# Attention scores as float32 products on quarters of the TensorE array, with queries and keys stored once

## The chip, the core and the metric

The kernel runs on one core of a Trainium2 chip. The metric is the device time of one execution in microseconds (us); lower is better. The core has a matrix engine (TensorE, PE in the profile; its weight loads are PEld), VectorE (DVE), ScalarE (ACT), GpSimd (POOL) and SyncE (SP), which issues the DMAs.

## What is computed

Windowed causal attention with a linear bias, and then a two-matrix feed-forward block on its output. B = 8 batches, H = 8 heads, S = 576 positions, D = 64; the feed-forward part has 4608 tokens, 512 features and 2048 inner features.

```python
scores = scale * np.matmul(q, k.transpose(0, 1, 3, 2))
mask = (rel >= 0) & (rel < 128)
scores = np.where(mask, scores + bias[None], -1000000000.0)
attn = softmax(scores)                      # over keys
x = np.matmul(attn, v)                      # heads joined: 4608 x 512
h = x @ w_in
g = h * erf(np.maximum(h, 0.0) + np.log1p(np.exp(-np.abs(h))))
return g @ w_out
```

## The kernel before

**A planner orders everything.** Each piece of work is an `op` with a cost per engine that may take it, the buffers that it reads and writes, and a due time `at`. `Plan.run` simulates the engines and the buffer slots and picks, on each engine, the ready op with the smallest due time. The kernel is emitted in that order. So a changed cost or buffer changes the order of all the work around it.

**Attention** runs as 48 spans: 12 chunks `c` of positions times 4 pairs of heads `g`. Every third chunk (16 spans, `w` = 1, the second kind) takes the last 192 positions of two batches; the other 32 spans (`w` = 0, the first kind) take 384 positions of one batch. A span has three tiles of 128 queries (two halves of 64). Each half sees three blocks of 64 keys (192 columns), in the first tile of a first-kind span two (128 columns).

- `operands` (DMA at L387) loads the span's queries and keys. Queries of the two halves lie on the diagonal of a 128x128 matrix whose other half is zeros, one such matrix for each head; the keys of half 0 lie on partitions 0 to 63, those of half 1 on 64 to 127. A key block that several tiles need is stored several times: 1792 or 1920 columns.
- `scores` (L422) makes two full-array products for each tile, one for each head, in float32, into one PSUM bank. VectorE adds the bias table and takes the row minimum of the negated scores (`biased`, L434), ScalarE takes the exponential and the sum (`exps`, L442).
- `normalise` divides (L465, GpSimd; VectorE too in the first four spans). `transpose_bank` transposes the probabilities on TensorE (L485), two banks a first-kind span and three a second-kind one, with a copy of each to SBUF (L403 on ScalarE, L407 on VectorE). `av` multiplies by the values into `px` (L501), and `px` is copied out by the same two lines and stored.

PSUM has eight banks: one each for scores (`s`), transposes (`t`) and `px` (`x`), and five that belong to the feed-forward part (`h` twice, `o0` to `o2`). In the first eight spans (`n < SPARE`) the scores of a tile take `s` or the two `h` in turn, and every second transposed bank takes `o1`.

**The feed-forward part** runs in two passes over the inner features. The first (7 of 16 blocks of weights) is interleaved with the attention, whose output it takes chunk by chunk; the second starts when the attention's SBUF memory has been given back. L694 makes `h`, L765 makes `o`; each product is split into three of a faster float format (high and low parts). L731 and L733 are its ScalarE functions. The weights are prepared on ScalarE and VectorE (L570 to L591). Warm-up products (L374) have the last due time and fill gaps on TensorE in the first microseconds.

Of the kernel before, what the change touches and what calls it, by code (L numbers as in the profile page):

```python
# [8 lines left out]
F32 = mybir.dt.float32  # L9
# [9 lines left out]
NPAIR = H // 2  # L19
P = 128  # L20
# [21 lines left out]
PB, XB, OB, TB = 8, 3, 3, 4  # L42
QB, VB = 4, 2

TE, NE = 2.0, 28
TA = 1.8
LL, LP, LT = 15, 6, 0
# [11 lines left out]
    [(2, 128), (3, 0), (3, 0)],  # L59
    [(3, 0), (3, 0), (3, 0)],  # L60
]
BANKS = [
# [5 lines left out]
]  # L68
VALUES = [
# [239 lines left out]
def dma(nbytes, n=1, us=0.475):  # L309
    return dict(costs={"SP": n * us}, moved=nbytes)  # L310
# [19 lines left out]
class Attention:  # L330
# [46 lines left out]
    def operands(self, c, g, w, at):  # L377

        op, sync, n = self.plan.op, self.nc.sync.dma_start, self.n
        x = Buf(self.qkp, [P, 1920], F32, "qk", QB, f"qk{n}")  # L380
        pos, parts = [0], []
        for blocks, _ in TILES[w]:
            pos.append(pos[-1] + 256 + 128 * blocks)
            parts.append(Part(x, slice(None), slice(pos[-2], pos[-1])))
        for a, b in ((0, 1), (1, 2), (2, 3)) if n < 2 else ((0, 3),):
            at += 0.01 * a
            op(emit=lambda e, a=pos[a], b=pos[b]: sync(x[:, a:b], self.src_qk[c, g, :, a:b]), w=parts[a:b], at=at,  # L387
               **dma(P * (pos[b] - pos[a]) * 4))
        self.loaded.append(Buf(ap=True))
        self.loaded[-1].writer = self.plan.ops[-1]  # L390
        return parts

    def values(self, c, g, w, at):

# [11 lines left out]
        else:  # L406
            self.nc.vector.tensor_copy(out, src)  # L407

    def scores(self, g, w, t, x, low, total, at):
        nc, op = self.nc, self.plan.op  # L410
        blocks, c0 = TILES[w][t]
        n = 64 * blocks
        nm = f"{self.n}_{t}"
        ways = [(self.ps, "s", 1)]
        if self.n < SPARE and t < 3:
            ways += [(self.spare[0], "h", 2)] * 2
        pool, tag, bufs = ways[self.step % len(ways)]
        ps = Buf(pool, [P, 2, 256], F32, tag, bufs, f"s{nm}")

        def products(e):  # L420
            for j in range(2):
                nc.tensor.matmul(  # L422
                    ps[:, j, :n], lhsT=x[:, j * P : (j + 1) * P], rhs=x[:, 2 * P + j * n : 2 * P + (j + 1) * n],
                    start=True, stop=True,
                )

        op({"PE": 2 * fp32_us(n)}, products, r=[x], w=[ps], at=at)
        pt = Buf(self.pp, [P, 3, 2, 64], F32, "p", PB, f"p{nm}")
        cut = lambda x: x.rearrange("p (c d) -> p c d", d=64)
        table = self.tables[g]  # L430

        def biased(e):
            for j in range(2):
                nc.vector.tensor_tensor_reduce(  # L434
                    out=pt[:, :blocks, j, :], in0=cut(ps[:, j, :n]), in1=cut(table.ap[:, j * 256 + c0 : j * 256 + c0 + n]),
                    scale=-0.125, scalar=3.0e38, op0=ALU.add, op1=ALU.min, accum_out=low[:, j : j + 1],
                )
# [7 lines left out]
        op({"DVE": 2 * (dve(n) + 0.05)}, biased, r=[ps, table], w=[pt, low], at=at)  # L445
        op({"Act": 2 * (act(n, 1) + 0.09)}, exps, r=[pt, low], w=[pt, total], at=at)
        return pt

# [60 lines left out]
    def span(self, c, g):  # L509
        op, n = self.plan.op, self.n  # L510
        w = int(c % 3 == 2)
        at = step_time(self.step) - LL + 0.01 * n
        x = self.operands(c, g, w, at)
        v = self.values(c, g, w, step_time(self.step) - LL + (VA if n < AHEAD else 2))
        p, totals = [], []
        st = Buf(self.pp, [P, 12], F32, "st", 4, f"st{n}")
        for t in range(3):
            at = step_time(self.step)
            low, total = (Part(st, slice(None), slice(k, k + 2)) for k in (2 * t, 6 + 2 * t))
            p.append(self.scores(g, w, t, x[t], low, total, at))  # L520
            totals.append(total)
            self.step += 1
        self.normalise(w, p, st, totals, at)
        at += LT
        sb = [Buf(self.ptp, [P, 512], F32, "pa", TB, f"pa{n}_{x}") for x in range(len(BANKS[w]))]
        for bi in range(len(BANKS[w])):
            self.transpose_bank(w, bi, p, sb, at)
        px = Buf(self.ps, [P, 512], F32, "x", 1, f"px{n}")
        for step in range(len(VALUES[w])):
            self.av(w, step, px, v, sb, at + 0.1)  # L530
        if c < DIRECT:
            xs = Part(self.moe.direct(c), slice(None), g, slice(0, CH))
# [321 lines left out]
def _layout(q, k, v, moe_w_in, moe_w_out):  # L854
    import numpy as np

    nb = q.shape[0]
    heads = lambda a: a.transpose(0, 1, 3, 2).reshape(nb, NPAIR, 2, D, S // 64, 64)
    qh, kh = heads(q), heads(k)
    vh = v.reshape(nb, NPAIR, 2, S // 64, 64, D)  # L860
    nc = 3 * nb // 2
    qk = np.zeros((nc, NPAIR, 2, D, 1920), q.dtype)
    vb = np.zeros((nc, NPAIR, 2, 64, 10, 2, D), v.dtype)
    for c in range(nc):
        x, y = 2 * (c // 3), 2 * (c // 3) + 1
        if c % 3 < 2:
            b = x + c % 3
            tiles = [((b, 2 * t, (2 * t - 1, 2 * t - 2, 2 * t)), (b, 2 * t + 1, (2 * t - 1, 2 * t + 1, 2 * t)))
                     for t in range(3)]
            tiles[0] = ((b, 0, (0, None)), (b, 1, (0, 1)))  # L870
            values = [(b, kb) for kb in range(6)]
        else:
            tiles = [((b, 6, (5, 4, 6)), (b, 7, (5, 7, 6))) for b in (x, y)]
            tiles.append(((x, 8, (7, 6, 8)), (y, 8, (6, 8, 7))))
            values = [(b, kb) for b in (x, y) for kb in range(4, 9)]
        pos = 0
        for halves in tiles:
            size = 64 * len(halves[0][2])
            for half, (b, qb, kbs) in enumerate(halves):
                for j in range(2):  # L880
                    at = pos + (2 * j + half) * 64
                    qk[c, :, half, :, at : at + 64] = qh[b, :, j, :, qb]
                    for n, kb in enumerate(kbs):
                        if kb is not None:
                            at = pos + 256 + j * size + n * 64
                            qk[c, :, half, :, at : at + 64] = kh[b, :, j, :, kb]
            pos += 256 + 2 * size
# [8 lines left out]
    rel = np.concatenate([  # L896
        r + 64 - col, np.where(low, r + 128, r - 64) - col, r - col, np.where(low, -1, r - 64 - col),
    ], axis=1)
    bias = np.where((rel >= 0) & (rel < WIN), -4.0 * rel, -1e30)
    bias = np.concatenate([bias, bias / 2], axis=1).astype(np.float32)  # L900
    return {
        "qk": qk.reshape(nc, NPAIR, P, 1920), "v_b": vb.reshape(nc, NPAIR, P, 10, P), "w_in": wi.reshape(NF, P, DM),
        "w_out": wo.reshape(NF, P, DM), "bias": bias,
    }

# [17 lines left out]
```

## Time and profile before

| | |
|---|---|
| time, median of 3 runs | 1044.85 us (1044.11 to 1045.27) |
| profiled execution | 1045.25 us |
| its span | 1043.1 us |
| TensorE busy | 1031.8 us, 99% |
| ScalarE, VectorE, GpSimd busy | 61%, 53%, 14% |
| DMA traffic | 141.22 MB |

A busy share is the union of an engine's recorded instructions. TensorE's instructions overlap in the record, since it is pipelined and their ends are modelled; so the distance from start to start tells what one of them takes in a row, and its recorded duration tells more than that. "Idle before" a group, or a wait, names what was released last. The chain that ended last is followed back from the last instruction: at each step to what released it, or to the instruction before it on its engine.

### The profile page before, as it was taken

The page shows a single profiled execution, that of the slowest core. Times are in us where ns is not written, and L with a number is a line of the kernel's source. Part 1 is how long each engine was busy: PE and PEld are TensorE (multiplying, and loading weights), DVE is VectorE, ACT ScalarE, POOL GpSimd, SP SyncE. Part 2 cuts the span into 40 slices and gives each one's busy share as a digit, 9 for nine tenths or more (in the row PEclk, how much of TensorE's full clock was granted, in tenths as well). Part 3 has the DMA queues.
Part 4 walks back from the last instruction along what each step waited for, and adds up shares of the span by engine and source line. Part 5 has one row for each costly group of instructions (what it writes and reads, how often), then busy time and mean ns, then how long its engine had stood idle before and what let it go on. Part 6 is the DMA issues. An engine that isn't in the chain of part 4 may idle for free.

```text
span 1043.1 us, 15075 instructions
## 1 busy us (share of the span) xinstructions
PE 1031.8 (99%) x5444; PEld 912.8 (88%) x5444; DVE 550.1 (53%) x1347; ACT 641.1 (61%) x1304; POOL 147.4 (14%) x274
## 2 busy tenths in 40 slices
PE   9999999999999999999999999999999999999998
PEld 8998999899999999999998888888888888888886
DVE  6989655535536535648237963443443535344252
ACT  6979965756755756758468866354454544535462
POOL 0633414323323223300000100000000000000000
PEclk9999999999999999999999999999999999999999
DMA  9987785545565464344112511213030303212011
GB/s 358 390 296 261 249 286 170 194 153 193 201 196 185 144 209 137 124 159 134 56 61 72 172 61 41 81 41 108 14 122 1 121 17 105 71 51 81 0 61 41
DMA packets 52697, 141.22 MB, mean 135 GB/s; under 512 B 5136, under 2 KB 20496, under 8 KB 52624
## 3 DMA queue, kind: packets, MB, share of 16 engines
q1 hardware_dynamic: 52624, 140.27, 39.6%
q8 instruction: 43, 0.70, 0.3%
q14 instruction: 30, 0.25, 0.1%
HBM read 111.94 MB, written 28.31 MB: 134 GB/s over the span
## 4 chain that ended last, share of the span: by engine, by line
PE 81%; ACT 9%; DVE 4%; DMA 2%; POOL 2%; issue 1%; SPq 0%; DVEq 0%; POOLq 0%; ACTq 0%
PE o L765 34%; PE h L694 32%; PE px L501 6%; PE s L422 5%; PE t L485 3%; ACT p L442 2%; POOL p L465 2%; ACT s L731 1%; ACT s L733 1%; ACT L733 1%; ACT L731 1%; ACT L735 1%; DMA xr<-xd 1%; DMA wro<-w_out 1%; ACT pa L403 1%
## 5 line engine op out<-in xcount | busy, mean ns | idle before, releaser
L694 PE MATMUL h<-xh,whi 128*128 128x384 f32 (+1 forms) x660 | 246.4, 373 | 0.3 <-ACT hs L676 0.3
L694 PE MATMUL h<-xh,wli 128*128 128x384 f32 (+1 forms) x660 | 239.4, 363 | 0.0
L694 PE MATMUL h<-xl,whi 128*128 128x384 f32 (+1 forms) x660 | 239.0, 362 | 0.0
L765 PE MATMUL o<-who,gh 128*128 128x512 f32 x576 | 234.4, 407 | 0.1
L765 PE MATMUL o<-who,gl 128*128 128x512 f32 x576 | 225.5, 392 | 0.0
L765 PE MATMUL o<-wlo,gh 128*128 128x512 f32 x576 | 225.2, 391 | 0.0
L676 ACT COPY hs<-h 128x384 f32<-128x384 f32 (+2 forms) x130 | 59.5, 468 | 237.4 <-PE h L694 237.2
L465 POOL TENSOR_SCALAR p<-p,st 128x192 f32<-128x192 f32 (+1 forms) x264 | 142.0, 557 | 299.4 <-DVE st L456 161.1
L442 ACT ACTIVATE p<-p,st 128x192 f32<-128x192 f32 (+1 forms) x288 | 124.8, 437 | 41.4 <-DVE st L434 41.0
L434 DVE CUSTOM_DVE_ANT_0 p<-s,tables 128x192 f32<-128x192 f32 (+1 forms) x288 | 86.1, 338 | 105.3 <-PE s L422 97.1
L694 PEld LDWEIGHTS h<-xh,whi 128*128 128x128 f32 x660 | 124.2, 188 | 15.4 <-ACT hs L676 0.7
L694 PEld LDWEIGHTS h<-xl,whi 128*128 128x128 f32 x660 | 124.2, 188 | 14.5
L694 PEld LDWEIGHTS h<-xh,wli 128*128 128x128 f32 x660 | 123.9, 188 | 12.6
L680 DVE COPY hs<-h 128x512 f32<-128x512 f32 (+2 forms) x63 | 36.4, 578 | 179.5 <-PE h L694 161.9
L765 PEld LDWEIGHTS o<-who,gl 128*128 128x128 f32 x576 | 108.2, 188 | 23.1
L765 PEld LDWEIGHTS o<-who,gh 128*128 128x128 f32 x576 | 108.4, 188 | 18.8 <-DVE ot L680 0.5
L765 PEld LDWEIGHTS o<-wlo,gh 128*128 128x128 f32 x576 | 108.5, 188 | 18.4
L422 PE MATMUL s<-qk 128*128 128x192 f32 (+1 forms) x576 | 111.3, 319 | 2.6 <-DMA qk<-qk 1.4
L501 PE MATMUL px<-pa,v 128*128 128x192 f32 (+2 forms) x704 | 107.2, 296 | 0.0
L501 PEld LDWEIGHTS px<-pa,v 128*128 128x128 f32 x704 | 103.2, 191 | 1.5 <-issue 0.3
L743 DVE TENSOR_TENSOR hs<-s,hs 128x768 f32<-128x768 f32 (+1 forms) x106 | 90.8, 887 | 21.4 <-ACT s L733 21.4
L422 PEld LDWEIGHTS s<-qk 128*128 128x128 f32 x576 | 90.1, 191 | 7.0 <-DMA qk<-qk 1.9
(58 smaller groups left out, 1040.8 us busy)
## 6 DMA issues: line engine op xcount, KB each, us to landing
qk<-qk SPq DMA_DIRECT2D x30, 896.0 KB, 6.6
qk<-qk SPq DMA_DIRECT2D x16, 960.0 KB, 6.8
v<-v_b SPq DMA_DIRECT2D x32, 384.0 KB, 4.5
xr<-xd SPq DMA_DIRECT2D x16, 768.0 KB, 4.9
v<-v_b SPq DMA_DIRECT2D x16, 640.0 KB, 4.4
pd<-ot SPq DMA_DIRECT2D x36, 256.0 KB, 4.6
ot<-pd SPq DMA_DIRECT2D x36, 256.0 KB, 3.4
wri<-w_in SPq DMA_DIRECT2D x16, 512.0 KB, 4.9
```

What stands on the lines that cost most here:

```text
L422: nc.tensor.matmul(ps[:, j, :n], lhsT=x[:, j * P : (j + 1) * P], rhs=x[:, 2 * P + j * n : 2 * P + (j + 1) * n], start=True, stop=True,)
L434: nc.vector.tensor_tensor_reduce(out=pt[:, :blocks, j, :], in0=cut(ps[:, j, :n]), in1=cut(table.ap[:, j * 256 + c0 : j * 256 + c0 + n]), s ...
L442: nc.scalar.activation(dst, dst, AF.Exp, bias=low[:, j : j + 1], scale=-1.0, accum_out=total[:, j : j + 1])
L465: (nc.vector if e == "DVE" else nc.gpsimd).tensor_scalar(dst, dst, totals[t][:, j : j + 1], 1.0, op0=ALU.mult, op1=ALU.mult)
L485: nc.tensor.matmul(cut[:, a : b + 1 : b - a], lhsT=p[t][:, kb].rearrange("p j d -> p (j d)"), rhs=self.ident[:, :], is_transpose=True, sta ...
L501: self.nc.tensor.matmul(dst[:, to : to + size], lhsT=v[:, blk], rhs=sb[s][:, off : off + size], start=(step + n == 0), stop=(last and n == ...
L676: self.nc.scalar.copy(out, src)
L680: self.nc.vector.tensor_copy(out, src)
L694: nc.tensor.matmul(ps[:, :W], lhsT=ww[:, cs], rhs=xx[:, k], start=(k2 + k + n == 0), stop=(k2 + k + n == 4),)
L731: A.activation(s[:, :n], hs[:, :n], AF.Softplus)
L743: op({"DVE": dve(n)}, lambda e, s=s, hs=hs, n=n: V.tensor_tensor(hs[:, :n], s[:, :n], hs[:, :n], ALU.mult), r=[s, hs], w=[hs], at=at)
L765: nc.tensor.matmul(po.all, lhsT=gg[:, cs], rhs=w.all, start=(u["start"] and n == 0), stop=(u["end"] and n == 2),)
```

## The change

Queries and keys are stored once for each span (768 or 1024 columns), head 0 of the pair on partitions 0 to 63 and head 1 on 64 to 127. A score product takes 64 partitions (one head) and 64 queries (one half): head and half choose a quarter of the array. The two heads of a tile write to two banks, the two halves to partitions 0 to 63 and 64 to 127 of each. Where the three key blocks of a half aren't neighbours in the right order, its product is cut into two segments of 64 and 128 columns. The order of the key blocks in a tile is adapted (`BANKS`, the bias table).

All three tiles of a first-kind span are one op of TensorE with one pair of banks; a second-kind span has two such ops (two tiles, then one), each with its pair; the first two spans have one op for each tile. The planner charges such an op `TURN` = 0.34 and half of what the streaming of its columns was charged before. The score banks are now two (`s` with two slots; two `h` for every second span among the first eight). `px` loses its own bank: it takes `o0` in the first eight spans and after that the bank `t` of the transposes.

```diff
+TURN, TS = 0.34, 0.0
+QUERIES = [(128, 0, 640), (0, 128, 256)]
+PIECES = [[(128, 384)], [(0, 128), (384, 512)], [(512, 768)]]
+KEYS = [
+    [[[(256, 0, 2)], [(256, 0, 2)]],
+     [[(256, 0, 3)], [(448, 0, 1), (320, 1, 2)]],
+     [[(384, 0, 3)], [(576, 0, 1), (448, 1, 2)]]],
...
+GROUPS = [[(0, 1, 2)], [(0, 1), (2,)]]
...
     def operands(self, c, g, w, at):
...
-        x = Buf(self.qkp, [P, 1920], F32, "qk", QB, f"qk{n}")
...
-        for a, b in ((0, 1), (1, 2), (2, 3)) if n < 2 else ((0, 3),):
...
+        size = 1024 if w else 768
+        x = Buf(self.qkp, [P, 1024], F32, "qk", QB, f"qk{n}")
+        pieces = PIECES if n < 2 else [[(0, size)]]
...
-    def scores(self, g, w, t, x, low, total, at):
+    def scores(self, w, x, ready, at):
+
+        nc, op = self.nc, self.plan.op
+        tiles = []
+        groups = [(0,), (1,), (2,)] if self.n < 2 else GROUPS[w]
+        banks = None
+        for group in groups:
+            if banks is None or w:
+                pool, tag = self.ps, "s"
+                if self.n < SPARE and self.n % 2:
+                    pool, tag = self.spare[0], "h"
+                banks = [Buf(pool, [P, 512], F32, tag, 2, f"s{self.n}_{group[0]}_{j}") for j in range(2)]
+                pos = 0
+            new = []
+            for t in group:
+                n = 64 * TILES[w][t][0]
+                new.append([Part(b, slice(None), slice(pos, pos + n)) for b in banks])
+                pos += n
+
+            def products(e, group=group, new=new):
+                for t, part in zip(group, new):
+                    q0 = QUERIES[w][t]
+                    for half, segments in enumerate(KEYS[w][t]):
+                        rows = slice(64 * half, 64 * half + 64)
+                        for k0, to, n in segments:
+                            for j in range(2):
+                                d = slice(64 * j, 64 * j + 64)
+                                nc.tensor.matmul(
+                                    part[j].all[rows, 64 * to : 64 * (to + n)],
+                                    lhsT=x[d, q0 + 64 * half : q0 + 64 * half + 64], rhs=x[d, k0 : k0 + 64 * n],
+                                    start=True, stop=True,
+                                )
+
+            op({"PE": TURN + sum(2 * (64 * TILES[w][t][0] / 1200.0 + 0.003) for t in group)}, products,
+               r=ready[group[-1]], w=[p for y in new for p in y], at=at + TS * group[0])
+            tiles += new
+        return tiles
+
+    def softmax(self, g, w, t, ps, low, total, at):
...
-        ways = [(self.ps, "s", 1)]
-        if self.n < SPARE and t < 3:
-            ways += [(self.spare[0], "h", 2)] * 2
-        pool, tag, bufs = ways[self.step % len(ways)]
-        ps = Buf(pool, [P, 2, 256], F32, tag, bufs, f"s{nm}")
-
-        def products(e):
-            for j in range(2):
-                nc.tensor.matmul(
-                    ps[:, j, :n], lhsT=x[:, j * P : (j + 1) * P], rhs=x[:, 2 * P + j * n : 2 * P + (j + 1) * n],
-                    start=True, stop=True,
-                )
-
-        op({"PE": 2 * fp32_us(n)}, products, r=[x], w=[ps], at=at)
...
     def span(self, c, g):
...
-        px = Buf(self.ps, [P, 512], F32, "x", 1, f"px{n}")
+        pool, tag = (self.spare[1], "o0") if n < SPARE else (self.ps, "t")
+        px = Buf(pool, [P, 512], F32, tag, 1, f"px{n}")
```

## Rows read from the trace of the kernel before

**Rows 1.** The page, parts 1 and 2: engines, and slices of TensorE and DMA.
```profile
PE 1031.8 (99%) x5444; PEld 912.8 (88%) x5444; DVE 550.1 (53%) x1347; ACT 641.1 (61%) x1304; POOL 147.4 (14%) x274
...
PE   9999999999999999999999999999999999999998
...
DMA  9987785545565464344112511213030303212011
```

**Rows 2.** The page, part 4: the chain that ended last, by engine and line.
```profile
PE 81%; ACT 9%; DVE 4%; DMA 2%; POOL 2%; issue 1%; SPq 0%; DVEq 0%; POOLq 0%; ACTq 0%
PE o L765 34%; PE h L694 32%; PE px L501 6%; PE s L422 5%; PE t L485 3%; ACT p L442 2%; POOL p L465 2%; ACT s L731 1%; ACT s L733 1%; ACT L733 1%; ACT L731 1%; ACT L735 1%; DMA xr<-xd 1%; DMA wro<-w_out 1%; ACT pa L403 1%
```

**Rows 3.** Windows: stretch, its length, busy time by engine, clock, DMA.
```profile
core 0: us, PE busy (x) PEld busy (x) DVE busy (x) ACT busy (x) POOL busy (x), PEclk, DMA share, GB/s
0.00:25.00 25.00, 22.44 (x153) 21.55 (x154) 15.39 (x92) 15.72 (x54) 0.70 (x6) 1.00 0.93 355
25.00:50.00 25.00, 24.60 (x175) 24.06 (x173) 23.40 (x100) 24.77 (x87) 14.62 (x27) 1.00 1.00 393
...
200.00:250.00 50.00, 49.18 (x299) 45.31 (x298) 26.47 (x97) 32.89 (x97) 19.93 (x36) 1.00 0.52 171
...
700.00:800.00 100.00, 100.00 (x443) 82.86 (x442) 43.84 (x58) 48.20 (x59) 0.00 (x0) 1.00 0.19 64
```

**Rows 4.** The chain in order of time, first 115 us: start, length, what.
```profile
0.74 0.40 SPq L387
...
11.11 1.78 PE warm_ps L374 x16
...
25.96 4.17 ACT p L442 x20
...
58.46 6.93 DMA wro<-w_out
...
102.51 7.37 DMA xr<-xd
```

**Rows 5.** Windows of line 422 alone: stretch, length, PE and PEld busy.
```profile
0.00:100.00 100.00, 31.55 (x167) 25.37 (x168) 1.00 0.89 325
```

**Rows 6.** The chain in order of time, 112 to 200 us.
```profile
131.56 0.44 PE t L485 x4
132.00 0.45 PE s L422 x4
...
134.27 1.69 PE px L501 x12
...
138.85 0.65 PE s L422 x4
```

**Rows 7.** Timeline of TensorE's products from 212.5 us: start, recorded length, what.
```profile
212.61 0.82 PE L422 MATMUL s<-qk 128*128 128x192 f32 x4
213.13 0.47 PE L694 MATMUL h<-xh,whi 128*128 128x384 f32 x1
213.44 0.34 PE L694 MATMUL h<-xl,whi 128*128 128x384 f32 x1
```

**Rows 8.** Line 422: min/median/max duration in ns, first and last start.
```profile
L422 PE MATMUL s<-qk x576: 270/326/430, 4.2 to 436.5; 128*128 128x192 f32 x128, 128*128 128x128 f32 x64
```

**Rows 9.** Timeline of all engines from 181.1 us; these products have 64 columns, then 128.
```profile
181.00 0.97 PEld L501 LDWEIGHTS px<-pa,v 128*128 128x128 f32 x8
```

**Rows 10.** Groups by line and shape: count, busy us, mean ns, idle before.
```profile
L434 DVE CUSTOM_DVE_ANT_0 p<-s,tables 128x192 f32<-128x192 f32 x224 | 70.5, 353 | 90.6 <-PE s L422 83.9 <-PE t L485 3.2 <-POOL p L465 2.7
...
L403 ACT COPY pa<-t 128x512 f32<-128x512 f32 x32 | 18.7, 586 | 10.5 <-PE t L485 10.4
...
L403 ACT COPY xs<-px 128x384 f32<-128x384 f32 x29 | 13.8, 476 | 31.2 <-PE px L501 27.6 <-issue 2.1 <-ACT p L442 1.1
```

**Rows 11.** Waits of TensorE's loads: us in total, times, longest.
```profile
PEld t L485 <- POOL p L465: 3.3, 7, 1.1
PEld t L485 <- ACT pa L403: 3.0, 7, 0.9
```

**Rows 12.** The page, part 6: DMA issues, KB each, us to landing.
```profile
qk<-qk SPq DMA_DIRECT2D x30, 896.0 KB, 6.6
qk<-qk SPq DMA_DIRECT2D x16, 960.0 KB, 6.8
```

More of the change, by code (lines that the diff above doesn't have):

```diff
@@ L61 @@
 ]
-BANKS = [
[5 rows of a table removed]
+QUERIES = [(128, 0, 640), (0, 128, 256)]
+PIECES = [[(128, 384)], [(0, 128), (384, 512)], [(512, 768)]]
+KEYS = [
[6 rows of a table added]
+]
+GROUPS = [[(0, 1, 2)], [(0, 1), (2,)]]
+BANKS = [
[5 rows of a table added]
 ]
@@ L379, in operands @@
         op, sync, n = self.plan.op, self.nc.sync.dma_start, self.n
-        x = Buf(self.qkp, [P, 1920], F32, "qk", QB, f"qk{n}")
[L381 to L384, printed above, removed]
-        for a, b in ((0, 1), (1, 2), (2, 3)) if n < 2 else ((0, 3),):
-            at += 0.01 * a
-            op(emit=lambda e, a=pos[a], b=pos[b]: sync(x[:, a:b], self.src_qk[c, g, :, a:b]), w=parts[a:b], at=at,
-               **dma(P * (pos[b] - pos[a]) * 4))
+        size = 1024 if w else 768
+        x = Buf(self.qkp, [P, 1024], F32, "qk", QB, f"qk{n}")
+        pieces = PIECES if n < 2 else [[(0, size)]]
+        parts = []
+        for k, piece in enumerate(pieces):
+            parts.append([Part(x, slice(None), slice(a, b)) for a, b in piece])
+            for (a, b), part in zip(piece, parts[-1]):
+                op(emit=lambda e, a=a, b=b: sync(x[:, a:b], self.src_qk[c, g, :, a:b]), w=[part],
+                   at=at + 0.01 * min(k, 1) + 0.01 * (k > 1), **dma(P * (b - a) * 4))
         self.loaded.append(Buf(ap=True))
         self.loaded[-1].writer = self.plan.ops[-1]
-        return parts
+        return x, [[p for y in parts[: k + 1] for p in y] for k in range(3)]
     def values(self, c, g, w, at):
@@ L434, in biased @@
                 nc.vector.tensor_tensor_reduce(
-                    out=pt[:, :blocks, j, :], in0=cut(ps[:, j, :n]), in1=cut(table.ap[:, j * 256 + c0 : j * 256 + c0 + n]),
+                    out=pt[:, :blocks, j, :], in0=cut(ps[j].all), in1=cut(table.ap[:, j * 256 + c0 : j * 256 + c0 + n]),
                     scale=-0.125, scalar=3.0e38, op0=ALU.add, op1=ALU.min, accum_out=low[:, j : j + 1],
@@ L443, in exps @@
                     dst, dst, AF.Exp, bias=low[:, j : j + 1], scale=-1.0, accum_out=total[:, j : j + 1])
-        op({"DVE": 2 * (dve(n) + 0.05)}, biased, r=[ps, table], w=[pt, low], at=at)
+        op({"DVE": 2 * (dve(n) + 0.05)}, biased, r=[*ps, table], w=[pt, low], at=at)
         op({"Act": 2 * (act(n, 1) + 0.09)}, exps, r=[pt, low], w=[pt, total], at=at)
@@ L512, in span @@
         at = step_time(self.step) - LL + 0.01 * n
-        x = self.operands(c, g, w, at)
+        x, ready = self.operands(c, g, w, at)
         v = self.values(c, g, w, step_time(self.step) - LL + (VA if n < AHEAD else 2))
@@ L516, in span @@
         st = Buf(self.pp, [P, 12], F32, "st", 4, f"st{n}")
+        ps = self.scores(w, x, ready, step_time(self.step))
         for t in range(3):
@@ L519, in span @@
             low, total = (Part(st, slice(None), slice(k, k + 2)) for k in (2 * t, 6 + 2 * t))
-            p.append(self.scores(g, w, t, x[t], low, total, at))
+            p.append(self.softmax(g, w, t, ps[t], low, total, at))
             totals.append(total)
@@ L861, in _layout @@
     nc = 3 * nb // 2
-    qk = np.zeros((nc, NPAIR, 2, D, 1920), q.dtype)
+    qk = np.zeros((nc, NPAIR, 2, D, 1024), q.dtype)
     vb = np.zeros((nc, NPAIR, 2, 64, 10, 2, D), v.dtype)
@@ L867, in _layout @@
             b = x + c % 3
-            tiles = [((b, 2 * t, (2 * t - 1, 2 * t - 2, 2 * t)), (b, 2 * t + 1, (2 * t - 1, 2 * t + 1, 2 * t)))
-                     for t in range(3)]
-            tiles[0] = ((b, 0, (0, None)), (b, 1, (0, 1)))
+            order = [(qh, b, 2), (qh, b, 3), (qh, b, 0), (qh, b, 1), *((kh, b, n) for n in range(6)), (qh, b, 4), (qh, b, 5)]
             values = [(b, kb) for kb in range(6)]
         else:
-            tiles = [((b, 6, (5, 4, 6)), (b, 7, (5, 7, 6))) for b in (x, y)]
-            tiles.append(((x, 8, (7, 6, 8)), (y, 8, (6, 8, 7))))
+            order = [(qh, x, 6), (qh, x, 7), (qh, y, 6), (qh, y, 7), (qh, x, 8), (qh, y, 8)]
+            order += [(kh, b, n) for b in (x, y) for n in range(4, 9)]
             values = [(b, kb) for b in (x, y) for kb in range(4, 9)]
[L876 to L887, printed above, removed]
+        for n, (src, b, block) in enumerate(order):
+            qk[c, :, :, :, n * 64 : n * 64 + 64] = src[b, :, :, :, block]
         for n, (b, kb) in enumerate(values):
@@ L896, in _layout @@
     rel = np.concatenate([
-        r + 64 - col, np.where(low, r + 128, r - 64) - col, r - col, np.where(low, -1, r - 64 - col),
+        np.where(low, r + 128, r - 64) - col, r + 64 - col, r - col, np.where(low, -1, r - 64 - col),
     ], axis=1)
@@ L901, in _layout @@
     return {
[L902 removed]
+        "qk": qk.reshape(nc, NPAIR, P, 1024), "v_b": vb.reshape(nc, NPAIR, P, 10, P), "w_in": wi.reshape(NF, P, DM),
         "w_out": wo.reshape(NF, P, DM), "bias": bias,
```

13 rows, old and new, of tables (BANKS, KEYS) are left out of this document.

## Prediction

> **What bounds the kernel now.** I read the page's engine shares and slices first [rows 1]. TensorE is busy 1031.8 us of a 1043.1 us span and its line of slices holds nines and a last eight; VectorE and ScalarE stand near 60%. Busy time of a pipelined engine can hide gaps, so the chain that ended last comes next [rows 2]: 81% of it is TensorE, and the scores (L422) are 5% of the span in it. The windows then separate the stages [rows 3]. From 200 us to 800 us TensorE is full and no other computing engine is above two thirds. In the first 50 us it is different: the DMA share is 0.93 and 1.00, and ScalarE is busy 24.77 of 25 us in the second window. The chain in order of time says the same of the start [rows 4]: 16 warm-up products stand in it at 11.11 us (products that nobody needs, put where TensorE had nothing else), from 25.96 us it runs through ScalarE, and later through a weight load of 6.93 us and a load of x of 7.37 us. So after some 110 us TensorE time is span, one for one; before that it is only partly so. About 14 of the 48 attention spans (167 score instructions at 12 a span) fall in the first 100 us [rows 5].
>
> The profiled execution took 1045.25 us, its span 1043.1 us, so 2.15 us lie around it; the median of the runs is 1044.85 us, 0.4 us lower. I sum against 1045.25 us.
>
> **The change part by part.** *The products themselves.* A float32 product is two TensorE instructions here: 288 products in the code (48 spans, three tiles, two heads), 576 in the trace [rows 8]. Four of them, one tile of both heads, take 0.45 us in the chain at 128 columns and 0.65 us at 192 [rows 6], 163 ns an instruction in the second case. A span of the first kind (tiles of 128, 192 and 192 columns, 32 such) costs 0.45 + 0.65 + 0.65 = 1.75 us, one of the second kind (three of 192, 16 such) 1.95 us; together 56.0 + 31.2 = 87.2 us. In them half of the stationary matrix is zero: two query halves lie on a diagonal. The change gives each head and each query half a quarter of the array. If the four quarters stream at once, a tile costs two instruction lengths in place of four: 87.2 / 2 = **43.6 us** go. No quarter product is in the trace, so the bounds are this saving and none at all (the quarters one after the other, which is the first rival). I take the full one, for the four write to different partitions or different banks, read different rows or feed different columns, and nothing they share is seen to be full: the new second segment of a half moves the same number of columns in total as the one it splits.
>
> *The turns.* Before the first quarter product and after the last one the array changes its arrangement. The change groups a span's tiles so that this happens once in a first-kind span, twice in a second-kind one and three times in the first two spans: 2 x 3 + 30 x 1 + 16 x 2 = 68 turns. Between score products and the next full-array product no gap exists now: four products from 212.61 us stream until 212.61 + 0.65 = 213.26 us, and the second h product starts at 213.44, one product length later [rows 7]. What a turn would expose is the tail of a product: a 192-column one is recorded as 326 ns [rows 8] and streams in 163, so 163 ns (an estimate, since recorded ends are modelled) lie between its last column and its end. Bounds: nothing, and two such tails, one in and one out, 0.33 us. I take two tails, as the work in front must leave before and the quarters after: 68 x 0.33 = **22.4 us** come back. The planner in the diff charges 0.34 us for a group, which is a constant of its model and no measurement. The Trainium skill, "TensorEngine Tiling (Array Packing)", Key Properties, says that a change of tiling mode drains the engine. No run so far shows a change of mode; without the rule the lower bound of nothing would be the nearer one and the forecast 22 us lower.
>
> *Weight loads.* Their count grows from 576 to 32 x 32 + 16 x 36 = 1600 (16 or 18 products a span, two instructions each). Full-width loads beside short products come no faster than (0.97 - 0.19) / 7 = 111 ns apart [rows 9]. A load of 64 columns is not in the trace; bounds 0 (under the other quarters' streams) and 56 ns (half of 111) each. I take 0, as loads beside products of 192 columns add little now (64 more columns cost (0.65 - 0.45) / 4 = 50 ns an instruction [rows 6], so 150 of the 163 ns are columns); the other end is a rival.
>
> *Banks.* Scores get two banks for a whole span; transposes and px now share one. The shared one holds, in a first-kind span, transposes 0.44, copy 0.59, the same again, px 1.69, copy 0.48: 4.2 us [rows 6, 10] and what passes between engines; a third bank makes it some 1.5 us more in a second-kind span. The score pair holds half of 1.75 us of products plus six VectorE passes of 0.35 us, about 3 us. A span comes every (436.5 - 4.2) / 48 = 9.0 us [rows 8]. So both fit, and what TensorE runs meanwhile is the first pass of the feed-forward part; were that cover gone, each of the 40 spans after the eighth would expose up to one copy, 0.59 us. I put it at zero, since TensorE's loads wait only 3.0 us for such copies in the whole run, where transposes share one bank already [rows 11]. Copies, biased passes, exps and scaling keep their sizes and numbers.
>
> *Loads.* A span's q and k shrink from 896 or 960 KB [rows 12] to 384 or 512 KB (768 or 1024 columns of 128 rows). The first tile of the first two spans waits for 128 KB and not 256. That relieves the one stretch in which the DMA is full, and there only. Each of the first two spans issues four loads in place of three; on SP's queue the bias, v and weight loads stand behind them, by some 0.4 us each (estimated as the 0.40 us of an issue) [rows 4], paid for by the smaller transfers.
>
> *The early stage.* The first 14 spans bring 2 x (0.88 - 1.0) + 6 x 0.55 + 4 x 0.32 + 2 x 0.55 = 5.4 us of the net gain. The chain there is ScalarE's and the DMA's, so freed TensorE time can turn into warm-ups; the lighter loads pull the other way. I count half, so **2.7 us** are lost.
>
> Sum: 1045.25 - 43.6 + 22.4 + 2.7 = 1026.8, **1027 us**.
>
> **The rivals.** (1) *The quarters don't overlap, since the two instructions of one float32 product need the same quarter.* The code issues head 0, then head 1, each product as two neighbouring instructions. If instructions start strictly in order, the second of a pair waits one length, 163 ns, for the first, and the next quarter's first stands behind it. Only the second of one and the first of the next run together: four products take four lengths, what two full-array products (four instructions) take now. The saving is nothing and the turns are paid: 1045.25 + 22.4 = 1068 us, slower; at one tail a turn 1056. For it: on the full array every start in the trace is in order. Against: there the products shared the whole array, so order cost nothing. It decides wherever the overlap saves less than 22.4 of the 43.6 us. In "TensorE: Matmul & The Clock Gate", The mechanism, the Trainium skill says that matmuls start and end strictly in order while different tiles run together 4 ns apart; no run here shows either for pairs, and read to the letter it gives this rival.
>
> (2) *Weight loads set the pace.* At 56 ns a load, 1600 take 89.6 us against 87.2 us now: no saving, turns paid, 1070 us. At half that, 44.8 us, they stay level with the streams and the forecast holds. For it: the 111 ns floor [rows 9]. Against: a load may run under three other quarters.
>
> (3) *The shared bank or the early stage keeps the gain.* 40 copies exposed at 0.59 us are 23.6 us, and with the whole 5.4 us lost early it is 1045.25 - 43.6 + 22.4 + 5.4 + 23.6 = 1053 us; with half the copies exposed 1041. For it: the longer hold of banks. Against: a 9.0 us period over some 4 to 6 us of use.
>
> (4) *Cheap turns.* One tail each: 68 x 0.163 = 11.1 us, so 1015 us. None, the early loss being 5.4: 1007 us.
>
> **How the numbers follow.** Forecast 0.58, its own range 1016 to 1038. Rival 1: 0.16, of it 0.05 near one tail. Rival 2: 0.07. Rival 3: 0.10 (0.04 faster, 0.03 the same, 0.03 slower). Rival 4: 0.09. A measurement of this kernel tells 0.2%, 2 us, from no change. Faster 0.58 + 0.09 + 0.04 = 0.71, the same 0.03, slower 0.16 + 0.07 + 0.03 = 0.26. The range runs from 1012 us (cheap turns, all but the cheapest) to 1058 us (rival 3's bad end and rival 1 at one tail); left out are the rest of rival 1, rival 2 and turns that cost nothing, about 0.2.
>
> **What would show it.** Timeline: a span's quarter products start in fours a few ns apart, and the group lasts about 0.88 us plus the turn; rival 1 shows starts a full 163 ns apart, rival 2 starts at a load's pace. The gap from the last score product to the next full one and the one ahead of the first show the turns: near 0.33 us together. L422's stretch of the chain shrinks from 87 to near 66 us with the turns. Waits of transposes and px for copies tell rival 3: more than 10 us of them would. The DMA share of the first 50 us falls well below 0.9, and the last score product starts near 420 us, not at 436.5 [rows 8]. The forecast is wrong if the granted clock, 1.00 in every window of [rows 3], falls in the first windows, where TensorE would be less filled: each microsecond of products at the lower level (1.2 GHz) would take two.

## The result and the profile after

| | median | against the kernel before on the same chip |
|---|---|---|
| before | 1044.69 us (1044.11 to 1045.27) | |
| after | 1029.42 us (1029.15 to 1029.63) | ratio 0.9854 (95% interval 0.9837 to 0.9871) |

The change takes 15.3 us away; the forecast was 1027 us, 17.7 us under that median. The span of the profiled execution fell from 1043.1 to 1027.4 us.

The page of the changed kernel, parts 1, 2, 4 and 6 (lines are shifted: scores L448, transposes L521, px L537, h L732, o L803):

```profile
span 1027.4 us, 17078 instructions
PE 1013.1 (99%) x6468; PEld 868.6 (85%) x6468; DVE 543.2 (53%) x1343; ACT 640.3 (62%) x1308; POOL 132.7 (13%) x274
...
DMA  8777563545353553164103420303031212212011
...
PE 87%; ACT 6%; DVE 3%; DMA 2%; issue 1%; POOL 0%; SPq 0%; ACTq 0%; DVEq 0%
PE o L803 37%; PE h L732 35%; PE px L537 7%; PE s L448 4%; PE t L521 4%; ACT p L478 1%; DMA wri<-w_in 1%; ACT pa L415 1%; DMA wro<-w_out 1%; ACT s L769 1%; ACT s L771 0%; POOL p L501 0%; DMA qk<-qk 0%; DMA xd<-xr 0%; ACT L771 0%
...
qk<-qk SPq DMA_DIRECT2D x30, 384.0 KB, 3.8
...
qk<-qk SPq DMA_DIRECT2D x16, 512.0 KB, 4.8
```

TensorE's busy time fell by 18.7 us against [rows 1], while its idle time (the span less the busy time) rose from 11.3 to 14.3 us. VectorE's and ScalarE's busy times hardly moved, and TensorE's share of the chain rose from 81% [rows 2] to 87%. The loads of queries and keys have shrunk as forecast, from the sizes of [rows 12] to 384 and 512 KB, and land in 3.8 and 4.8 us, not 6.6 and 6.8.

The timeline of TensorE's products in the changed kernel, around one first-kind span that lies between an h and an o product (start, recorded length, what, count):

```profile
199.43 0.34 PE L732 MATMUL h<-xh,wli 128*128 128x384 f32 x1
199.70 1.12 PE L448 MATMUL s<-qk 64*64 64x128 f32 x32
200.75 0.50 PE L803 MATMUL o<-who,gh 128*128 128x512 f32 x1
201.09 0.39 PE L803 MATMUL o<-wlo,gh 128*128 128x512 f32 x1
```

Two product lengths from the same trace turn this into a cost: in a row, an h product of 384 columns takes 174 ns from start to start, an o product 227 ns. The h ends its stream at 199.43 + 0.174 = 199.60, and the second o starts at 201.09, so the first one streamed from 200.86. The group took 1.26 us in between. Its columns need half of the old 1.75 us, 0.875, so **0.385 us** are the turn, the change of the array to quarters and back. The kernel before has no such gap [rows 7]. The 32 product instructions stand on 64 rows by 64 columns of the array, the quarters of the change. In the same timeline cut off at 199.75 us and at 199.9 us, four of them have begun at once (the trace has their starts 7 ns apart), and eight within 0.2 us:

```profile
199.70 0.34 PE L448 MATMUL s<-qk 64*64 64x128 f32 x4
...
199.70 0.45 PE L448 MATMUL s<-qk 64*64 64x128 f32 x8
```

Full-array products of 128 columns start 0.45 / 4 = 112 ns apart [rows 6], so eight took 0.9 us. Line 448 as a whole (durations in ns, first and last start) has 1600 instructions, as counted, and its last product starts at 418.9 us, not at 436.5 [rows 8]; the forecast said near 420.

```profile
L448 PE MATMUL s<-qk x1600: 216/272/473, 3.9 to 418.9; 64*64 64x128 f32 x79, 64*64 64x64 f32 x50, 64*64 64x192 f32 x49
```

Windows of the two kernels, first before, then after (stretch, length, busy time by engine, clock, DMA share, GB/s):

```profile
0.00:100.00 100.00, 95.71 (x639) 91.14 (x640) 82.86 (x306) 83.47 (x248) 34.93 (x60) 1.00 0.89 325
```

```profile
0.00:100.00 100.00, 91.26 (x971) 81.09 (x972) 86.20 (x318) 85.34 (x256) 33.58 (x60) 1.00 0.78 261
100.00:450.00 350.00, 349.75 (x2912) 306.21 (x2911) 180.38 (x648) 239.65 (x641) 94.33 (x210) 1.00 0.46 143
```

In the first 100 us TensorE is now idle 8.7 us and not 4.3, while the DMA share fell from 0.89 to 0.78 (on the page, from 9 and 9 tenths in the first two slices to 8 and 7); from 100 to 450 us TensorE is full. The clock stays at 1.00 (2.4 GHz).

### The profile page after: what moved, and what is told of

The parts are those of the page before. It is cut to its first block, busy times and chain, and to the rows that moved or that the text cites. A ratio compares the mean times of both kernels' runs of the same rounds, so it can differ in the third digit from the quotient of the medians.

```text
span 1027.4 us, 17078 instructions
## 1 busy us (share of the span) xinstructions
PE 1013.1 (99%) x6468; PEld 868.6 (85%) x6468; DVE 543.2 (53%) x1343; ACT 640.3 (62%) x1308; POOL 132.7 (13%) x274
## 4 chain that ended last, share of the span: by engine, by line
PE 87%; ACT 6%; DVE 3%; DMA 2%; issue 1%; POOL 0%; SPq 0%; ACTq 0%; DVEq 0%
PE o L803 37%; PE h L732 35%; PE px L537 7%; PE s L448 4%; PE t L521 4%; ACT p L478 1%; DMA wri<-w_in 1%; ACT pa L415 1%; DMA wro<-w_out 1%; ACT s L769 1%; ACT s L771 0%; POOL p L501 0%; DMA qk<-qk 0%; DMA xd<-xr 0%; ACT L771 0%
## 5 line engine op out<-in xcount | busy, mean ns | idle before, releaser
L732 PE MATMUL h<-xh,whi 128*128 128x384 f32 (+1 forms) x660 | 244.4, 370 | 0.3 <-ACT hs L714 0.3
L732 PE MATMUL h<-xh,wli 128*128 128x384 f32 (+1 forms) x660 | 239.5, 363 | 0.0
L732 PE MATMUL h<-xl,whi 128*128 128x384 f32 (+1 forms) x660 | 239.0, 362 | 0.0
L803 PE MATMUL o<-who,gh 128*128 128x512 f32 x576 | 230.8, 401 | 0.2
L803 PE MATMUL o<-who,gl 128*128 128x512 f32 x576 | 225.6, 392 | 0.0
L803 PE MATMUL o<-wlo,gh 128*128 128x512 f32 x576 | 225.2, 391 | 0.0
L501 POOL TENSOR_SCALAR p<-p,st 128x192 f32<-128x192 f32 (+1 forms) x264 | 127.2, 501 | 300.1 <-DVE st L492 230.1
L732 PEld LDWEIGHTS h<-xh,whi 128*128 128x128 f32 x660 | 124.1, 188 | 17.8 <-issue 1.7
L732 PEld LDWEIGHTS h<-xl,whi 128*128 128x128 f32 x660 | 124.1, 188 | 14.8
L478 ACT ACTIVATE p<-p,st 128x192 f32<-128x192 f32 (+1 forms) x288 | 124.4, 437 | 17.7 <-DVE st L470 17.5
L732 PEld LDWEIGHTS h<-xh,wli 128*128 128x128 f32 x660 | 123.8, 188 | 12.6
L803 PEld LDWEIGHTS o<-who,gl 128*128 128x128 f32 x576 | 108.1, 188 | 23.0
L803 PEld LDWEIGHTS o<-who,gh 128*128 128x128 f32 x576 | 108.3, 188 | 22.1 <-issue 2.1
L470 DVE CUSTOM_DVE_ANT_0 p<-s,tables 128x192 f32<-128x192 f32 (+1 forms) x288 | 82.6, 337 | 82.0 <-PE s L448 77.1
L803 PEld LDWEIGHTS o<-wlo,gh 128*128 128x128 f32 x576 | 108.4, 188 | 18.8
L537 PEld LDWEIGHTS px<-pa,v 128*128 128x128 f32 x704 | 99.9, 191 | 8.5 <-ACT pa L415 4.6
L537 PE MATMUL px<-pa,v 128*128 128x192 f32 (+2 forms) x704 | 103.2, 299 | 2.2 <-ACT pa L415 1.1
L785 DVE TENSOR_TENSOR gl<-hs,gh 128x768 fp32r<-128x768 f32 (+1 forms) x106 | 90.9, 885 | 6.1 <-ACT gh L714 5.3
L769 ACT ACTIVATE s<-hs 128x768 f32<-128x768 f32 (+1 forms) x106 | 76.4, 776 | 0.5
```

The lines of the kernel that those rows point to most:

```text
L470: nc.vector.tensor_tensor_reduce(out=pt[:, :blocks, j, :], in0=cut(ps[j].all), in1=cut(table.ap[:, j * 256 + c0 : j * 256 + c0 + n]), scal ...
L478: nc.scalar.activation(dst, dst, AF.Exp, bias=low[:, j : j + 1], scale=-1.0, accum_out=total[:, j : j + 1])
L501: (nc.vector if e == "DVE" else nc.gpsimd).tensor_scalar(dst, dst, totals[t][:, j : j + 1], 1.0, op0=ALU.mult, op1=ALU.mult)
L537: self.nc.tensor.matmul(dst[:, to : to + size], lhsT=v[:, blk], rhs=sb[s][:, off : off + size], start=(step + n == 0), stop=(last and n == ...
L732: nc.tensor.matmul(ps[:, :W], lhsT=ww[:, cs], rhs=xx[:, k], start=(k2 + k + n == 0), stop=(k2 + k + n == 4),)
L769: A.activation(s[:, :n], hs[:, :n], AF.Softplus)
```

## Experiments

| run | median, us | ratio to before (95% interval) |
|---|---|---|
| e1_twice | 1067.15 | 1.0218 (1.0203 to 1.0233) |
| e2_quarter_major | 1065.06 | 1.0197 (1.0182 to 1.0212) |
| e3_full_between | 1065.45 | 1.0206 (1.0190 to 1.0221) |
| e4_full_ahead | 1041.67 | 0.9977 (0.9963 to 0.9990) |
| e5_full_loads | 1038.55 | 0.9942 (0.9928 to 0.9955) |
| e6_before_shared | 1049.88 | 1.0049 (1.0037 to 1.0062) |
| e7_turn38 | 1029.56 | 0.9856 (0.9843 to 0.9870) |
| e8_late_full_loads | 1030.16 | 0.9863 (0.9850 to 0.9877) |
| e9_loads_earlier | 1028.19 | 0.9837 (0.9823 to 0.9850) |
| e10_due_times | 1023.64 | 0.9799 (0.9786 to 0.9813) |
| e11_before_due | 1045.51 | 1.0013 (1.0000 to 1.0026) |

### Do the quarters stream at once? Every product twice

```diff
+                for again in range(2):
-                for t, part in zip(group, new):
+                    for t, part in zip(group, new):
...
```

> The changed kernel with every quarter product of a group issued a second time, into the same place, inside the same group: streaming doubles, the number of turns stays, the plan and the order of the work stay. Theory (four quarters stream at once, a turn is paid for a group and not for a product): plus 32 x 0.853 + 16 x 0.96 = 42.7 us by columns, so some 1072 us, and each group is longer by its streaming alone (0.85 or 0.64 or 0.32 us). Rival 1 (the two instructions of a product keep the quarters apart): plus about 87 us, 1116 us. Rival 2 (weight loads set the pace, 1600 more of them at 56 ns): plus 90 us, 1119 us.

Measured: 1067.15 us, 37.7 us above the changed kernel. The timeline of this run, the same kind of place:

```profile
201.96 0.34 PE L733 MATMUL h<-xh,wli 128*128 128x384 f32 x1
202.23 2.01 PE L449 MATMUL s<-qk 64*64 64x128 f32 x64
204.17 0.50 PE L804 MATMUL o<-who,gh 128*128 128x512 f32 x1
204.51 0.39 PE L804 MATMUL o<-wlo,gh 128*128 128x512 f32 x1
```

By the same working the group takes 204.51 - 0.227 - (201.96 + 0.174) = 2.15 us: 0.89 more for 32 more product instructions and as many more weight loads. That is what the columns over four quarters need (0.875). Quarters held apart as in the first rival would add 1.75 us, and 32 loads at 56 ns 1.8 us. So the quarters overlap, the loads cost nothing beyond the streams, and the first two rivals fall. In all, the doubled streaming is 43.6 us by columns, and TensorE's busy time rose by 42.9 us, to 1056.0. But the time rose by only 37.7, some 5 us less than the 1072 us expected: the idle time fell from 14.3 to 9.2 us. The windows say where (this run):

```profile
0.00:100.00 100.00, 96.50 (x1373) 88.62 (x1374) 80.18 (x303) 79.28 (x241) 27.95 (x57) 1.00 0.76 240
```

TensorE idles 3.5 us in the first 100 us, 5.2 less than in the changed kernel. Some 5 us of TensorE time there are free; the rest of the 12.7 us that the first 14 spans add (ten of 0.875, four of 0.975) is paid.

### Does the order of issue matter? Quarter by quarter

```diff
-                for t, part in zip(group, new):
-                    q0 = QUERIES[w][t]
-                    for half, segments in enumerate(KEYS[w][t]):
-                        rows = slice(64 * half, 64 * half + 64)
-                        for k0, to, n in segments:
-                            for j in range(2):
-                                d = slice(64 * j, 64 * j + 64)
+                for half in range(2):
+                    rows = slice(64 * half, 64 * half + 64)
+                    for j in range(2):
+                        d = slice(64 * j, 64 * j + 64)
+                        for t, part in zip(group, new):
+                            q0 = QUERIES[w][t]
+                            for k0, to, n in KEYS[w][t][half]:
...
```

> The changed kernel with the products of a group issued quarter by quarter (all tiles of half 0 and head 0, then half 0 and head 1, and so on) in place of head by head within each segment; same products, same count, same plan. If each quarter takes its own work from a queue that looks far enough ahead, the issue order costs little: 1029 to 1035 us. If instructions start in the order of issue, each quarter runs alone: streaming is four times as long, plus 32 x 2.56 + 16 x 2.88 = 128 us, 1157 us; something between tells how far the look ahead reaches.

Measured: 1065.06 us, 35.6 us above the changed kernel: between the two theories. The timeline of this run:

```profile
200.08 0.34 PE L732 MATMUL h<-xh,wli 128*128 128x384 f32 x1
200.35 2.26 PE L448 MATMUL s<-qk 64*64 64x128 f32 x32
202.54 0.50 PE L803 MATMUL o<-who,gh 128*128 128x512 f32 x1
202.88 0.39 PE L803 MATMUL o<-wlo,gh 128*128 128x512 f32 x1
```

The same 32 instructions now take 2.40 us, 1.14 more. Each quarter alone would add three times 0.875, 2.6 us. So work for a free quarter is found behind work for a busy one, though not without limit.

The single starts in the trace give the limit; their widths tell the quarters apart. The first quarter's third instruction of six starts at 200.617 us and the second quarter's first at 200.623, while the first quarter's fourth, issued ahead of it, starts only at 200.779. The third quarter begins 6 ns after the second's third of six, the fourth 6 ns after the third's seventh of ten. In the two-tile groups of the second kind (4, 4, 8 and 8 instructions) the second and third quarters begin at once and the fourth 5 ns after the third's fifth of eight. Each time, three instructions of a busy quarter are still to start: three can wait there, and a fourth holds up all behind it. The trace shows the first pattern in all 29 groups of 32 instructions, the second in 15 of 16 groups of 24. The two instructions of one product are too few for that, so the first rival's order doesn't arise; neighbours in the issue order should go to different quarters.

### What is a turn worth? Full-array products between the tiles, and ahead of them

```diff
+                    if t != group[0]:
+                        nc.tensor.matmul(
+                            part[0].all[:, :64], lhsT=x[:, 128:256], rhs=x[:, 256:320], start=True, stop=True)
```

In the first run this stands inside the loop over the tiles, just before a tile's own products; in the second, all of them stand ahead of the loop.

> The changed kernel with one full-array float32 product of 64 columns between the tiles of a group (its result is overwritten by the tile's own product): two more turns in each of 30 first-kind spans and one in each of 16 second-kind ones, 76 in all; 76 x 0.17 us for the products themselves. To be read against the run with the same 76 products ahead of the group. Theory (a turn costs 0.33 to 0.38 us): 25 to 29 us above that run, some 1068 to 1071 us. Rival (turns are cheap, one tail or none): 0 to 12 us above it.

> The control: the same 76 full-array products of 64 columns as in the run with products between the tiles, all issued ahead of the group, so that no turn is added. 76 x 0.17 = 13 us more than the changed kernel, 1042 us, under every theory of the turn.

Measured: 1065.45 and 1041.67 us. The control lies 12.3 us above the changed kernel (13 expected), and 76 added turns cost 23.8 us more, **0.31 us a turn**, a little under the 25 to 29 us expected. TensorE's busy time differs by more, 1053.3 against 1027.7 us, which is 0.34 us a turn; the idle time took up 3.2 us. The timelines, first with the products between, then ahead:

```profile
200.98 0.34 PE L735 MATMUL h<-xh,wli 128*128 128x384 f32 x1
201.25 0.45 PE L451 MATMUL s<-qk 64*64 64x128 f32 x8
201.62 0.43 PE L443 MATMUL s<-qk 128*128 128x64 f32 x2
201.99 0.57 PE L451 MATMUL s<-qk 64*64 64x192 f32 x12
202.49 0.43 PE L443 MATMUL s<-qk 128*128 128x64 f32 x2
202.85 0.56 PE L451 MATMUL s<-qk 64*64 64x192 f32 x12
...
203.68 0.40 PE L806 MATMUL o<-wlo,gh 128*128 128x512 f32 x1
```

```profile
205.74 0.33 PE L736 MATMUL h<-xh,wli 128*128 128x384 f32 x1
205.91 0.55 PE L443 MATMUL s<-qk 128*128 128x64 f32 x4
206.39 1.12 PE L452 MATMUL s<-qk 64*64 64x128 f32 x32
207.44 0.50 PE L807 MATMUL o<-who,gh 128*128 128x512 f32 x1
207.78 0.39 PE L807 MATMUL o<-wlo,gh 128*128 128x512 f32 x1
```

From the end of the h stream to the start of the first o stream (the second o's start less 227 ns) the first takes 2.30 us, the second 1.64: 0.33 us for each of the two added turns. The cheap-turn rival falls.

### What are the smaller loads worth?

```diff
-        size = 1024 if w else 768
+        size = 1920 if w else 1792
...
+        if n < 2:
+            part = Part(x, slice(None), slice(768, size))
+            op(emit=lambda e: sync(x[:, 768:size], self.src_qk[c, g, :, 768:size]), w=[part], at=at + 0.02,
+               **dma(P * (size - 768) * 4))
```

> The changed kernel, but each span loads as many bytes as before the change (1792 or 1920 columns; the ones beyond 768 or 1024 are zeros that nothing reads, and in the first two spans they come last). The products are the changed kernel's. Theory of the prediction (the smaller loads win back about half of the early loss, 2.7 us): 1031 to 1034 us. If the loads are hidden anyway: 1029 us. If the early stage hangs on the DMA: 1036 us or more, and the additional time lies in the first 100 us.

Measured: 1038.55 us, 9.1 us above the changed kernel, over three times the 2.7 us that the prediction in effect credited to them. The timeline of TensorE in this run, with its idle time and what ended it, and a window, first of this run, then of the changed kernel:

```profile
82.15 0.34 PE L736 MATMUL h<-xh,wli 128*128 128x384 f32 x1
84.46 0.33 PE L525 MATMUL t<-ident,p 128*128 128x128 f32 x1 [1.98 <-POOL p L505]
85.86 0.48 PE L525 MATMUL t<-ident,p 128*128 128x128 f32 x1 [1.07 <-POOL p L505]
87.88 0.69 PE L525 MATMUL t<-ident,p 128*128 128x128 f32 x2 [1.54 <-POOL p L505]
```

```profile
75.00:100.00 25.00, 19.13 (x158) 16.64 (x158) 23.46 (x61) 23.44 (x58) 8.43 (x13) 0.86 0.75 249
75.00:100.00 25.00, 23.34 (x216) 20.49 (x206) 23.55 (x63) 24.39 (x56) 8.95 (x12) 1.00 0.73 251
```

Here the plan has nothing else for TensorE while it waits for the scaled probabilities, 4.6 us in three waits, and within them the granted clock falls: 0.86 as the mean of the window, 1.2 GHz for part of it. This window alone holds 4.2 us more idle time than in the changed kernel, and the lower clock comes on top. The chain of this run goes there through VectorE, from 81 to 92 us mostly through its preparation of weights, behind which the sums for the scaling wait. The larger loads changed the planned order: TensorE's work beside the scores stands in another order than in the changed kernel from 11 us on. So much of the loss is one wait that the new order leaves without cover, and not a slow load in every span; how much each part costs was not measured by itself. To see whether later loads matter too:

```diff
-        size = 1024 if w else 768
+        size = (1920 if w else 1792) if n >= 14 else (1024 if w else 768)
...
```

> The changed kernel with the loads of the size of before from the fifteenth span on, and the small ones in the first fourteen. Theory (the 9.1 us that loads of the old size cost in all spans come from the first 100 us, where they keep the DMA full; afterwards they are hidden): 1029 to 1030 us. Rival (the larger loads cost TensorE something in every span, by traffic or by being late): of 9.1 us the 34 later spans would bring 34/48, some 1036 us.

Measured: 1030.16 us, 0.7 us above the changed kernel. Here TensorE's order is the changed kernel's throughout. Large loads in 34 of 48 spans are hidden; nearly all of the 9.1 us depend on the first 14.

### The shared bank, alone

```diff
-        px = Buf(self.ps, [P, 512], F32, "x", 1, f"px{n}")
+        pool, tag = (self.spare[1], "o0") if n < SPARE else (self.ps, "t")
+        px = Buf(pool, [P, 512], F32, tag, 1, f"px{n}")
```

> The kernel before with one part of the change alone: px takes o0 in the first eight spans and then the bank of the transposes. Theory (the shared bank fits in the 9.0 us of a span, and TensorE has other work): 1045 us, within 2 us of the kernel before. Rival 3 (each of 40 spans exposes a copy of 0.59 us or part of it): 1050 to 1068 us.

Measured, on the kernel before: 1049.88 us, **5.5 us slower** than before on the same chip. The waits of TensorE's weight loads, first in this run, then in the changed kernel:

```profile
PEld t L485 <- ACT pa L403: 4.9, 12, 0.6
PEld px L501 <- ACT pa L403: 2.4, 9, 0.4
...
PEld px L501 <- DVE pa L407: 1.9, 5, 1.1
```

```profile
PEld t L521 <- ACT pa L415: 8.4, 19, 0.9
PEld px L537 <- ACT pa L415: 4.6, 13, 0.8
...
PEld px L537 <- DVE pa L419: 2.3, 4, 1.3
```

Where transposes and px had waited 3.0 us for copies on ScalarE [rows 11], they wait 7.3 us here and 13.0 us in the changed kernel, px for the first time. From 100 us on, where TensorE is full, the waits for copies on both engines are 2.7 us in the kernel before, 8.2 us here and 9.0 us in the changed kernel. The 5.5 us more match the time lost here. (The planner's order moves with the edit, on TensorE from 69 us on.) That is the third rival's mechanism, at a fourth of its full price.

### The planner's charge and its due times

```diff
-TURN, TS = 0.34, 0.0
+TURN, TS = 0.38, 0.0
```

> The changed kernel with the planner's charge for a group set to 0.38 us, what a group costs beyond its streaming in the profile after. Only the order of the emitted work can change. If a wrong charge costs anything, 1 to 2 us are gained, 1027 to 1029 us; if not, 1029 to 1030 us.

Measured: 1029.56 us, the changed kernel's time. The charge needs no mending. Then the loads were made due earlier (`LL` from 15 to 24), alone and with other due times, both with the charge at 0.38:

```diff
-TURN, TS = 0.34, 0.0
-TE, NE = 2.0, 28
-TA = 1.8
-LL, LP, LT = 15, 6, 0
-TM = 1.2 * TA * 20 / (1.5 * NF1)
-LEAD = 70
+TURN, TS = 0.38, 0.0
+TE, NE = 1.72, 28
+TA = 1.56
+LL, LP, LT = 24, 6, 0
+TM = 4.05
+LEAD = 73
...
-MC, MP, MH = 0.01, 16, -16
-W1A, W1B, W1C = 20, 4, 0.3
+MC, MP, MH = 0.01, 16, -18
+W1A, W1B, W1C = 11, 4, 0.3
```

> The changed kernel with loads of queries, keys and values due 24 us and not 15 us ahead of their span, and the planner's charge for a group at 0.38 us. Theory (some 3 us of the change's gain are lost in the first 100 us, partly because first spans wait for loads, which are now small enough to come earlier): 1026 to 1028 us. If the early stage hangs on ScalarE and VectorE alone: 1029 to 1030 us.

> The same, with the other due times moved too (spans due every 1.72 and then 1.56 us a tile, first-pass units every 4.05 us from 73 us on, their weights 11 us ahead, h products 18 us ahead). Theory: more of the early loss comes back, 1024 to 1027 us; bound from below by the turns and the streaming, 1022 us. If due times matter no further than the loads: as the run with earlier loads.

Measured: 1028.19 us with earlier loads, some 1 us better, with overlapping intervals; **1023.64 us** with all due times moved, 5.8 us under the changed kernel and faster than both kernels. The window of the first 100 us in that run:

```profile
0.00:100.00 100.00, 96.53 (x1061) 87.96 (x1062) 84.65 (x344) 84.83 (x270) 41.05 (x77) 0.98 0.79 257
```

TensorE idles 3.5 us in the first 100 us in place of 8.7, at a clock that was at its lower level for a moment (0.98 as the mean). Over the whole span it idles 9.4 us in place of 14.3, which is nearly all of the 5.2 us between the spans of the two profiled runs. The control, the same due times in the kernel before:

> The kernel before, with the due times of the run with moved due times and nothing else of it. If those due times are worth as much without the change, the kernel before gains 5 us too, 1039 to 1041 us. If they are worth something only with the small loads and the shorter groups: 1043 to 1050 us.

Measured: 1045.51 us, no gain and perhaps 0.1% lost. So the freed 5 us are the change's own, left lying by the old due times. Which of the moved due times regains them, beyond the 1 us or so of the earlier loads, was not separated.

## Why the prediction was right, and where it was not

**The products: right.** Half of the streaming goes; the second set of products costs 0.89 us a span where the working gave 0.875. **The weight loads: right** at zero, with 1600 more of them in that run.

**The turns: right, a little small.** Two tails gave 0.33 us; in the trace after a turn is 0.385 us, and between tiles 0.31 to 0.34. At 0.385 the 68 turns are 26.2 us, not 22.4. The two ends aren't alike as supposed: in the group shown, the second four products start at 199.86 us, so the first four streamed from about 199.75, 0.14 us behind the h product, and some 0.2 us pass between the last quarter's columns and the o product. The Trainium skill's sentence that a change of tiling mode drains the engine ("TensorEngine Tiling (Array Packing)", Key Properties) agrees with this, with 0.31 us or more for a change there and back. The Trainium skill's rule that products start strictly in order ("TensorE: Matmul & The Clock Gate", The mechanism), which read to the letter gave the first rival, doesn't hold here: in quarter-major order the second quarter's first product starts at 200.623 us, before three of the first quarter's that were issued ahead of it. The measurement decides, and a span's 32 instructions took 1.26 us with the turn.

**The banks: wrong.** The step took zero, since loads waited 3.0 us for copies with transposes sharing a bank. That wait belonged to the old arrangement and said nothing of px, which had never waited. The third rival's price of 23.6 us held as an upper bound, and the part of it that is exposed is 5.5 us in the kernel before. The prediction's own sign for that rival, more than 10 us of such waits, did appear (13.0 us for ScalarE's copies alone, 4.8 of them in the first 100 us), though the gain stayed. That use fits into 9.0 us a span says nothing of how close together the uses lie: the code gives a span's transposes one due time and px one 0.1 us later, so each can find the copy before it unfinished. That this is the reason was not tested.

**The early stage: the mechanism was right, its size wrong in both directions.** The prediction lost half of 5.4 us there. Part of TensorE's time in that stretch is indeed worth nothing (some 5 us of extra products were absorbed). What the change freed there became idle time, not warm-ups, of which the traces hold 56 before and after. The lighter loads pull the other way as said, but by 9.1 us and not by 2.7, in part through the planned order.

Added up by what was measured: the 34 later spans save 43.6 less the first 14 spans' 12.7, so 30.9 us, and pay 46 turns, 17.7 us: -13.2. The loads bring -9.1, the bank +5.5 as in the kernel before, and early streaming and early turns nothing: -16.8 against a measured -15.3 us. In the prediction's own terms, the turns cost 3.8 us more and the bank 5.5 us more than it took, and the early stage, by what is left of the 15.3 us, brought some 3.4 us where it counted a loss of 2.7. So it was luck in part that the forecast lay only 2.4 us under the measured time: errors of 9.3 and 6.1 us stand against each other. What the bank costs inside the changed kernel was not measured by itself (all eight banks are taken there); the waits above, 9.0 us against 8.2, suggest about as much. Taking early streaming and turns as free is argued from the idle time, not shown, and holds for some 5 us at most: of the 12.7 us of early streaming that were added, more was paid than absorbed.

Three readings were off without bearing on the forecast. Between 200 and 800 us other engines do pass two thirds (ScalarE 37.93 of 50 us from 350 to 400 us, VectorE 43.83 of 50 from 550 to 600). The 87 us given for L422's stretch of the chain is its streaming in all; the chain held 5.3% of the span, 55 us, and holds 4.0%, 41 us, now. And the cheap-turn rival kept early losses of 2.7 and 5.4 us where half of the first 14 spans' gain would be 4.5 and 6.3, so 1017 and 1008 us.

## What to carry to other kernels

Before filling the array with smaller tiles, count the changes of arrangement: here the quarters halve 87 us of streaming, and 68 turns at 0.31 to 0.385 us take half of the saving back or a little more, so work of one arrangement belongs together, issued so that neighbours use different quarters. A bank that is shared must be priced by what the second user would newly wait for, not by the waits that the first one has. And when work on the bounding engine shrinks, move the due times with it: that was worth another 5.8 us here, and nothing without the change.

## What the runs showed of the hardware that was not expected

A queue of products finds work for a free quarter behind work for a busy one, but only so far: 2.40 us in quarter-major order against 1.26 alternating and some 3.9 (1.26 + 2.6) for quarters one after the other. In those starts three instructions can wait for a busy quarter, and a fourth holds up the rest.

And with loads of the old size the clock fell in the middle of the first stage: after a wait of 1.98 us and a single transpose, within the next wait of 1.07 us. The windows of 1 us have it at 1.00 from 84 to 85 us, at 0.74 in the next and at 0.50 from 86 to 92 us. The h products, 174 ns from start to start at the full clock, then stood 320 ns apart (windows and timeline of the run with full loads):

```profile
85.00:86.00 1.00, 0.14 (x1) 0.14 (x1) 0.86 (x2) 0.99 (x6) 1.00 (x2) 0.74 0.93 387
86.00:87.00 1.00, 0.34 (x1) 0.04 (x1) 1.00 (x2) 0.93 (x2) 1.00 (x1) 0.50 0.96 401
...
89.04 0.52 PE L736 MATMUL h<-xh,wli 128*128 128x384 f32 x1
89.36 0.52 PE L736 MATMUL h<-xh,whi 128*128 128x384 f32 x1
```
